# Strassen's seven products in the down-projection of a linear-attention and feed-forward layer, one Trainium2 core

## The chip, the core and the metric

The kernel runs on one core of a Trainium2 chip. Times are device microseconds (us) of one launch. The kernel before took 235.34 us (median of 3 runs, 234.85 to 235.41). The profile shows one further execution, whose instructions span 232.8 us. The 2.54 us between that span and the median lie around the instructions that the profile lists.

Five engines work side by side, each through its own queue in order: TensorE (PE, with its weight loads PEld), VectorE (DVE), ScalarE (ACT), GpSimd (POOL) and SyncE (SP), which here only issues DMAs.

## What is computed

The reference is one layer on 2048 tokens of width D = 640 in bf16: a pre-normed linear attention with 32 heads of 20, whose feature map is two softmaxes per head, and a pre-normed feed-forward block with F = 1728 hidden units.

```python
h = x + attention(layernorm(x), wqkv, w_phi, wo)
def _B_ref(x, w1, w2):
    h = jnp.einsum("bsd,df->bsf", x, w1)
    h = _silu(h)
    out = jnp.einsum("bsf,fd->bsd", h, w2)
    return out
h2 = h + _B_ref(_layernorm(h, axis=-1), B_w1, B_w2)
```

The change sits in the last product, silu(...) @ w2.

## The kernel before

The 2048 tokens are 16 tiles of 128. F is cut into 13 full chunks of 128 and a last one of 64. X stays in memory as 16 tiles of 128x640; the residuals are added into it.

**Order.** Nothing is scheduled while the program is built. Each piece of work is a named step (`add(name, emit)`, L212), and the list `ORDER` (L18 to L56) says in which order the steps are emitted (loop at L929). An engine gets its instructions in that order; between engines only data and buffers decide.

**Steps by name**, t being the tile. First half of the list: `K`, `V`, `kv` project keys and values and sum their products over all tiles. Then per tile: `Q` (L630, PE, 10 matmuls) projects queries, `qe` takes exponentials on ACT, `qs` sums them on DVE (L660), `qr` scales them on DVE (L690, from tile 6 on with a reciprocal L676 and ratio L682 before it), `qt` transposes by DMA (L702), `D` (L728) multiplies by the summed keys and values, `E` divides on DVE (two halves, L739), `ot` transposes by DMA, `G` (L764) is the output projection (two halves of 320 columns, 5 matmuls each), `ga` adds the residual on DVE (L772), `ls`, `lr`, `hn` are the layer norm: statistics on DVE (L430), the inverse root on POOL (L437, L443 and L446), the scaling on DVE (L448); `ht` transposes by DMA.

**Feed-forward.** The tiles are grouped in units: tiles 0 and 1, then 2 to 5, 6 to 9, 10 to 13, then 14 and 15 (L777). `u{a}.{f}` (L843) is an up-projection of the unit that starts at tile a: 5 matmuls of 512 columns for one hidden chunk of a unit of four tiles, or 10 of 256 for two chunks of a unit of two. `s` applies silu on ACT (L866) into the tile `shT`, hidden chunk by hidden chunk, tokens along the free axis. `u.L`, `s.L` and `lt` do the last 64 hidden units and transpose them. `d{t}{g}` (`ffn_down`, L884) is the down-projection of tile t for one half g of the 640 columns: 13 matmuls of 320 columns (L890) and one for the last 64 units (L893), accumulated in one bank. For tile 15 the second half is cut into 192 and 128 columns (`groups`, L807). `oa` (`ffn_out`, L895, L899) adds the bank and X on DVE into an output tile, of which there are two; `out` (L903) stores it.

**Banks.** From the step `halves` on (L706), the eight PSUM banks are handed out in a ring (`ps_half`, L121): a new use of a bank waits until the eighth use before it has been read.

**Memory.** The pool `late` (L837), which holds `shT` and the output tiles, takes the place of the pool `proj` (normalized rows, key, value and query weights) when the last exponentials `qe15` have been emitted. The key and value buffers EK and VP (L195, L197) lie in the pool `persist` and stay to the end.

Of the kernel before, what the change touches and what calls it, by code (L numbers as in the profile page):

```python
# [35 lines left out]
hn0 lr1 ot3 Q15 G20 hn1 ht1 qs6 G21 qe15 qs7 ht0 D5 G30 load8 pad1 ga20 qr6 ga21 ga30 G31 load11 E50 E51  # L36
D4 u0.12 E40 u0.4 u0.0 s0.0 s0.12 ga31 ls3 u0.6 E41 ot5 qs8 u0.L u0.2 ls2 qr7 s0.6 u0.8 qt6 lr2 s0.4 ot4
u0.10 D6 s0.L G50 s0.10 G40 lt0 qt7 lr3 s0.8 E60 G51 E61 s0.2 d10 ot6 ga40 hn2 ga50 ga51 ls5 hn3 lr5 G41
d00 D7 d01 ga41 ls4 G60 lr4 hn5 G61 E70 ht2 ht3 hn4 oa10 ht5 d11 qr8 oa00 ht4 ga61 u2.2 u2.0 ga60 qt8
E71 ot7 s2.0 oa01 qs9 u2.L qs13 s2.2 qr9 oa11 qs11 u2.6 D8 u2.10 E80 ls6 qt9 u2.7 u2.3 s2.L u2.11 s2.10  # L40
s2.6 qr13 E81 u2.9 s2.9 qr11 u2.5 qs12 s2.7 qs10 s2.3 u2.1 D9 G70 s2.5 E90 qr10 u2.12 s2.11 E91 ot8 G71
u2.4 lr6 ga71 ga70 qt11 out0 lt2 s2.1 qt10 u2.8 out1 hn6 s2.4 qr12 ls7 G80 s2.8 ga80 ot9 G81 D11 s2.12
E110 d30 ht6 qt13 E111 d20 D10 ga81 lr7 G90 E100 oa30 oa20 E101 ot10 G91 hn7 ga91 d31 ot11 ga90 ls8 qs15
lr8 d21 qt12 oa31 d50 G100 ls9 G101 hn8 out3 d40 d51 ht8 lr9 hn9 oa21 ga101 G110 out2 ga100 ga110 oa50
oa40 G111 qs14 d41 oa51 D12 ls10 ht7 E120 ht9 u6.1 u6.0 oa41 ga111 u6.12 u6.8 D13 s6.0 s6.1 qr14 s6.8
E121 s6.12 u6.11 ot12 u6.2 u6.3 qr15 lr10 s6.11 u6.L s6.2 E130 ls11 out4 E131 u6.9 qt15 s6.3 G120 ot13
s6.L u6.6 lt6 s6.6 lr11 u6.7 u6.10 hn10 u6.5 out5 s6.7 hn11 s6.9 u6.4 qt14 G121 ga120 ga121 s6.5 ht11
G130 D14 G131 E140 ga131 s6.10 s6.4 d60 ls12 oa60 d61 d70 ht10 lr12 E141 d91 ga130 ls13 oa61 hn12 oa70
D15 lr13 d90 ht12 ot14 d71 hn13 ht13 out6 G140 oa71 oa90 u10.L oa91 ga140 out9 E150 u10.0 u10.1 out7
E151 u10.6 G141 u10.9 s10.L s10.0 s10.6 u10.8 ga141 d80 u10.7 s10.1 u10.3 u10.11 ot15 s10.3 u10.5 u10.12  # L50
oa80 s10.9 s10.8 s10.11 u10.2 u10.4 ls14 s10.7 s10.5 u10.10 s10.12 s10.4 G150 G151 lt10 lr14 d81 s10.10
s10.2 d110 hn14 oa81 ht14 out8 d111 ga150 d120 ga151 ls15 d101 lr15 d100 hn15 oa100 oa110 ht15 oa101
d121 oa111 out10 oa120 out11 u14.L u14.4 u14.0 oa121 s14.0 s14.L u14.8 u14.6 s14.6 u14.2 d131 u14.12
# [6 lines left out]
def kernel(  # L60
# [151 lines left out]
    def add(name, emit):  # L212
        steps[name] = emit
# [680 lines left out]

    def ffn_out(t, g):  # L895
        if g == 0:
            outs[t] = pools["late"].tile([P, D], BF16, name="o_t", bufs=2)
        a, b = groups(t)[g]
        nc.vector.tensor_tensor(  # L899
            outs[t][:, a:b], ps_of.pop(("d", t, g))[:, 0 : b - a], X[:, t, a:b], op=ALU.add,  # L900
        )
# [24 lines left out]

    late = f"qe{T - 1}"
# [39 lines left out]
```

## Time and profile before

| what | value |
|---|---|
| median of 3 runs | 235.34 us |
| span of the profiled execution | 232.8 us |
| PE busy | 228.0 us, 1977 matmuls |
| DVE busy | 164.0 us, 340 instructions |
| ACT busy | 107.4 us, 241 instructions |
| POOL busy | 62.6 us, 99 instructions |
| down-projection matmuls of 320 columns (L890) | 403, 59.3 us |
| output additions of 320 columns (L899) | 31, 14.2 us |
| mean granted TensorE clock | 1.000 |

How to read it: each engine's share of the span is an average over stages. A matmul's own duration (299 ns for 320 columns) is longer than the distance to the next one, because matmuls are pipelined; what one costs in a row of them is the length of the row over its count. The chain that ended last leads back from the last instruction to whatever released each step. The windows show the busy time of each engine in a stretch of the span.

### The profile page before, as it was taken

Reading aid. Unit: us, or ns where it says so; the run is one execution under the profiler, and the core shown is the slowest. Engines: PE = TensorE matmul, PEld = TensorE weight load, DVE = VectorE, ACT = ScalarE, POOL = GpSimd, SP = SyncE. Lnnn points to the kernel's source line nnn. Section 1 sums busy time; section 2 is a strip of 40 time slices with the busy share of each in tenths; the row PEclk is TensorE's granted clock in tenths of the full one; section 3 lists DMA queues with packets and bytes.
Section 4 is the critical chain, followed back from the end, with each engine's and each line's share of the span. In section 5 each row is a group of like instructions: output and inputs, shape, how many; then the busy total and the mean of one; then the engine's idle time right before and its main releaser. Section 6 shows DMA issues by size and latency. Waiting matters only on the chain.

```text
span 232.8 us, 5040 instructions
## 1 busy us (share of the span) xinstructions
PE 228.0 (98%) x1977; PEld 160.5 (69%) x1984; DVE 164.0 (70%) x340; ACT 107.4 (46%) x241; POOL 62.6 (27%) x99
## 2 busy tenths in 40 slices
PE   7999999999999999999999999999999999999995
PEld 5777777777777778877545777655677455778874
DVE  4989999999999899998999794891472330404031
ACT  2899999998879884410344000064200235001400
POOL 7589896995001120211010111110020010100000
PEclk9999999999999999999999999999999999999999
DMA  6995379698836766696236956137213301011011
GB/s 169 336 291 103 87 119 217 217 145 188 220 115 114 159 116 136 124 121 146 56 66 154 120 114 158 30 80 172 55 28 85 99 0 28 31 28 56 8 56 56
DMA packets 67213, 26.79 MB, mean 115 GB/s; under 512 B 60151, under 2 KB 66167, under 8 KB 67063
## 3 DMA queue, kind: packets, MB, share of 16 engines
q1 hardware_dynamic: 66535, 26.47, 49.9%
q8 instruction: 15, 0.25, 0.5%
q10 hardware_dynamic: 656, 0.03, 0.2%
q14 instruction: 7, 0.06, 0.1%
HBM read 9.64 MB, written 2.62 MB: 53 GB/s over the span
## 4 chain that ended last, share of the span: by engine, by line
PE 95%; DMA 2%; SPq 1%; issue 1%; ACT 1%; DVE 0%
PE banks L890 24%; PE banks L850 24%; PE banks L498 18%; PE banks L536 9%; PE banks L767 9%; PE banks L589 2%; PE banks L734 2%; PE banks L893 2%; DMA Wk<-in_A_wqkv_dram 2%; PE banks L861 1%; PE banks L525 1%; PE banks L400 1%; ACT Wfk L325 1%; SPq L166 1%; PE banks L510 0%
## 5 line engine op out<-in xcount | busy, mean ns | idle before, releaser
L870 ACT ACTIVATE shT<-banks 128x512 bf16<-128x512 f32 (+1 forms) x53 | 28.5, 591 | 84.2 <-PE banks L850 84.2
L890 PE MATMUL banks<-w_sb,shT 128*128 128x320 bf16 (+2 forms) x429 | 61.3, 295 | 0.0
L850 PE MATMUL banks<-HnT,w_sb 128*128 128x512 bf16 (+1 forms) x318 | 58.4, 335 | 0.4
L890 PEld LDWEIGHTS <-shT 128*128 128x128 bf16 x429 | 41.1, 98 | 15.2
L850 PEld LDWEIGHTS <-w_sb 128*128 128x128 bf16 x325 | 31.2, 98 | 22.1
L899 DVE TENSOR_TENSOR o_t<-banks,X 128x320 bf16<-128x320 f32 (+2 forms) x33 | 14.9, 474 | 39.6 <-PE banks L893 26.7
L443 POOL TENSOR_SCALAR rs<-mv 128x1 f32<-128x1 f32 x21 | 5.8, 276 | 113.2 <-DVE mv L435 113.2
L498 PEld LDWEIGHTS <-XnT 128*128 128x128 bf16 x300 | 28.5, 98 | 10.3
L450 POOL TENSOR_SCALAR xn<-X,mv,rs 128x640 bf16<-128x640 bf16 x12 | 31.3, 2615 | 4.1 <-ACT rs L441 2.1
L434 DVE BATCH_NORM_STATS2 st<-X 128x6 f32<-128x320 bf16 x64 | 27.9, 477 | 4.3 <-DMA X<-in_A_x_dram 4.0
L767 PE MATMUL banks<-wo_sb,OT 128*128 128x320 bf16 x160 | 24.8, 299 | 0.0
L662 DVE TENSOR_REDUCE Sq<-EQ 128x66 f32<-128x1320 bf16 x16 | 23.9, 1512 | 0.0
L774 DVE TENSOR_TENSOR X<-banks,X 128x320 bf16<-128x320 f32 x32 | 14.7, 483 | 13.0 <-PE banks L767 12.9
L658 ACT ACTIVATE EQ<-banks 128x360 bf16<-128x360 f32 (+2 forms) x52 | 22.0, 514 | 3.2 <-PE banks L536 3.1
L557 DVE TENSOR_REDUCE Sk<-EK 128x64 f32<-128x1280 bf16 x16 | 23.3, 1468 | 0.2 <-ACT EK L553 0.2
L536 PE MATMUL banks<-Wfq,XnT 128*128 128x360 bf16 (+2 forms) x160 | 23.3, 299 | 0.0
L498 PE MATMUL banks<-Wv,XnT 128*128 128x320 bf16 x150 | 22.5, 299 | 0.0
L498 PE MATMUL banks<-Wfk,XnT 128*128 128x320 bf16 x150 | 22.5, 299 | 0.0
L553 ACT ACTIVATE EK<-banks 128x640 bf16<-128x640 f32 x32 | 20.5, 698 | 1.4 <-PE banks L498 1.2
L767 PEld LDWEIGHTS <-OT 128*128 128x128 bf16 x160 | 15.2, 98 | 6.5
L536 PEld LDWEIGHTS <-XnT 128*128 128x128 bf16 x160 | 15.2, 97 | 6.2
L747 DVE TENSOR_TENSOR O<-banks,Rd 128x360 bf16<-128x360 f32 (+1 forms) x32 | 15.7, 491 | 1.1
(76 smaller groups left out, 203.0 us busy)
## 6 DMA issues: line engine op xcount, KB each, us to landing
out_dram<-o_t SPq DMA_DIRECT2D x15, 160.0 KB, 2.0
w_sb<-in_B_w_dram SPq DMA_DIRECT2D x5, 432.0 KB, 4.8
w_sb<-in_B_w_dram SPq DMA_DIRECT2D x3, 480.0 KB, 4.1
X<-in_A_x_dram SPq DMA_DIRECT2D x1, 1280.0 KB, 8.4
Wk<-in_A_wqkv_dram SPq DMA_DIRECT2D x5, 160.0 KB, 3.8
Wv<-in_A_wqkv_dram SPq DMA_DIRECT2D x5, 160.0 KB, 4.9
wo_sb<-in_A_wo_dram SPq DMA_DIRECT2D x1, 800.0 KB, 6.5
X<-in_A_x_dram SPq DMA_DIRECT2D x1, 640.0 KB, 5.9
```

Of the source, the lines that this page charges most:

```text
L434: nc.vector.bn_stats(st[:, i, :], X[:, t, i * HD : (i + 1) * HD])
L450: eng.tensor_scalar(out=xn_[t][:], in0=X[:, t, :], scalar1=mv_.pop(t)[:, 0:1], scalar2=rs_.pop(t)[:], op0=ALU.subtract, op1=ALU.mult,)
L498: nc.tensor.matmul(ps[:, g, 0:HD], XnT[:, c, t * P : (t + 1) * P], W[:, c, g * HD : (g + 1) * HD], start=(c == 0), stop=(c == C - 1),)
L536: nc.tensor.matmul(ps[:, 0 : e - a], XnT[:, c, t * P : (t + 1) * P], Wfq[:, c, a:e], start=(c == 0), stop=(c == C - 1),)
L553: nc.scalar.activation(E5[:, :, :, b, :], p4, AF.Exp, scale=sign)
L557: nc.vector.tensor_reduce(sk[t][:], ek[t][:, 0 : H * HF].rearrange("p (q f) -> p q f", f=DH), axis=AX.X, op=ALU.add)
L658: nc.scalar.activation(features(t, a, b)[:, :, :, i], p4, AF.Exp, scale=sign)
L662: nc.vector.tensor_reduce(sq[t][:], EQ[0][:, t, :, 0:FCH].rearrange("p c (q f) -> p c q f", f=DH), axis=AX.X, op=ALU.add)
L767: nc.tensor.matmul(ps[:, 0:HD], ot[t][:, c, :], wo_sb[:, c, g * HD : (g + 1) * HD], start=(c == 0), stop=(c == C - 1),)
L850: nc.tensor.matmul(ps[:, at : at + n], w1_sb[:, c, fc * P : fc * P + P], HnT[u][:, c, 0:n], start=(c == 0), stop=(c == C - 1),)
L870: nc.scalar.activation(shT[u][:, f0 * n : f1 * n], ps_of.pop(("u", u, f0))[:, 0 : (f1 - f0) * n], AF.Silu)
L890: nc.tensor.matmul(ps[:, 0 : b - a], shT[u][:, at : at + P], w2_sb[:, fc, a:b], start=(fc == 0), stop=False,)
```

## The change

For tiles 2 to 15, taken in seven pairs, twelve of the thirteen full hidden chunks are multiplied by Strassen's scheme in Winograd's form. The two tiles are the two row blocks, chunks 0 to 5 and 6 to 11 the two inner blocks, columns 0 to 319 and 320 to 639 the two column blocks. Instead of eight block products (two tiles, two inner blocks, two column blocks) there are seven, `p1` to `p7`, of 6 matmuls each. The thirteenth chunk and the last 64 hidden units are multiplied as before (`rest`, at the end of p2, p3 and p4 and as `p8`). The seven products go into four banks, a to d, of which a takes p1, p6, p5 and a rest in turn and d takes p7 and p4; in between DVE reads the bank. Tiles 0 and 1 keep `d` and `oa`.

New work around the products:

- `T1` to `T4`, three steps each: sums of blocks of w2, once, on POOL, 128x640 each.
- `S1` to `S4` per pair: sums of blocks of `shT`, 128x768 each. S1 and S3 run on POOL, S2 and S4 on DVE; S2 needs S1, S4 needs S2. Each has one buffer.
- `r1`, `r2`, `r3`, `r7` per pair on DVE: bank plus X into an f32 tile of 128x320.
- `w11`, `w12`, `w21`, `w22` per pair on DVE: bank plus such a tile into the output tile.
- In the last pair p3 and w12 are cut at column 192 of the half; the stores of tile 14 come in three parts (columns 0 to 319, 320 to 511, 512 to 639), that of tile 15 in one.

There are four output tiles instead of two. VP and EK move into a pool that is closed together with `proj`. The list `ORDER` is rewritten from the step after `ga10` on; up to there it is the same.

```diff
-ga00 qe10 ga10 qt3 Q11 D3 qr4 qt5 ls0 G11 qe11 Q14 Q12 E30 Q13 lr0 ot2 qe14 ga11 qe12 qe13 ls1 qt4 E31
...
+ga00 qe10 ga10 qt3 Q11 D3 qr4 ot2 qt4 pad1 qt5 load11 ls0 G11 load8 qs7 qe11 Q14 qe14 lr0 Q12 G21 ga11
...
+lt0 lr5 hn2 ls4 hn5 ht2 E70 s0.8 ht5 ht3 u0.6 lr4 D8 E80 E71 T2.1 hn4 E81 s0.0 qs9 s0.6 d10 qr9 qs11
+T2.2 ht4 d11 d00 G60 oa10 G61 d01 u2.L T2.0 oa11 oa00 oa01 ot7 T3.0 s2.L qt9 ga61 u2.9 ga60 u2.0 u2.4
...
+qr13 ga111 qr12 S3.2 s2.11 p1.2 lr8 s2.10 qt13 p7.2 G110 r1.2 S1.2 S2.2 hn7 S3.4 r7.2 p6.2 out0 r2.2
+S4.2 p4.2 ht6 ga90 G100 ga91 w21.2 hn8 ls9 p5.2 qt12 G101 r3.2 p3.2 ga100 lr9 p8.2 ht8 ht7 S1.4 ga110
+hn9 p2.2 w22.2 D13 D12 ht9 ga101 w11.2 p2.4 E130 w12.2 ls10 p1.4 p7.4 u6.L r1.4 E131 S2.4 u6.2 S4.4 p6.4
...
+S4.10 lt14 r7.10 s14.10 p4.10 p5.10 S1.12 S3.12 r3.10 w21.10 p2.10 w11.10 p8.10 w22.10 s14.0 s14.8 p3.10
+S2.12 p1.12 s14.12 u14.6 r1.12 S4.12 s14.6 p7.12 out8 p6.12 p2.12 w12.10 S3.14 r7.12 r2.12 w11.12 p5.12
+r3.12 p4.12 p3.12 S1.14 S2.14 p1.14 p7.14 r1.14 p8.12 w21.12 out10 w22.12 p6.14 r7.14 r2.14 out11 p2.14
+w11.14 out140 p5.14 p4.14 S4.14 w12.12 p3.14x r3.14 p8.14 p3.14 out12 w21.14 w12.14x w22.14 w12.14 out13
+out142 out15 out141
...
+    keys = proj_ctx.enter_context(tc.tile_pool(name="keys", bufs=1, side="right"))
...
-    VP = [persist.tile([P, H, HV], BF16, name=f"VP{i}") for i in range(NV)]
-    EK = [persist.tile([P, FCH * (NCH - 1) + P], BF16, name=f"EK{i}") for i in range(NE)]
+    VP = [keys.tile([P, H, HV], BF16, name=f"VP{i}") for i in range(NV)]
+    EK = [keys.tile([P, FCH * (NCH - 1) + P], BF16, name=f"EK{i}") for i in range(NE)]
...
+    KS = (FC - 2) // 2
...
+    def weight_sum(k, c):
+        if k not in ws:
+            ws[k] = pools["late"].tile([P, KS, HD], BF16, name=f"T{k}")
+        (b11, b12), (b21, b22) = halves_of_w2()
+        x, y = {1: (b12, b11), 2: (b22, ws.get(1)), 3: (b22, b12), 4: (b21, ws.get(2))}[k]
+        part = slice(2 * c, 2 * c + 2)
+        nc.gpsimd.tensor_tensor(ws[k][:, part], x[:, part], y[:, part], op=ALU.subtract)
...
+    def token_sum(t, k):
+        S_[t, k] = pools["late"].tile([P, KS, P], BF16, name=f"S{k}", bufs=1)
+        a11, a12, a21, a22 = (block(t + i, j) for i in range(2) for j in range(2))
+        x, y, op = {
+            1: (a21, a22, ALU.add), 2: (S_.get((t, 1)), a11, ALU.subtract),
+            3: (a11, a21, ALU.subtract), 4: (a12, S_.get((t, 2)), ALU.subtract),
+        }[k]
+        eng = engines[on(f"S{k}.{t}", ("DVE", "POOL")[k % 2])]
+        eng.tensor_tensor(S_[t, k][:], x if k in (1, 3, 4) else x[:], y[:] if k == 4 else y, op=op)
+
+    FIRST = {1: "a", 2: "c", 3: "b", 7: "d"}
+    INTO = {1: "a", 2: "c", 3: "b", 4: "d", 5: "a", 6: "a", 7: "d"}
+    OTHER = {2: (0, 0), 3: (0, 1), 4: (1, 0)}
...
+    def product(t, k, lo=0, hi=HD):
+        bank = INTO[k] + "x" * (lo > 0)
+        if k in FIRST:
+            ps_of[bank, t] = ps_half()
+        ps = ps_of[bank, t]
+        (b11, b12), (b21, b22) = halves_of_w2()
+        left = {
+            1: lambda: block(t, 0), 2: lambda: block(t, 1), 3: lambda: S_[t, 4], 4: lambda: block(t + 1, 1),
+            5: lambda: S_[t, 1], 6: lambda: S_[t, 2], 7: lambda: S_[t, 3],
+        }[k]()
+        right = {1: b11, 2: b21, 3: b22, 4: ws.get(4), 5: ws.get(1), 6: ws.get(2), 7: ws.get(3)}[k]
+        for c in range(KS):
+            nc.tensor.matmul(
+                ps[:, lo:hi], left[:, c, :], right[:, c, lo:hi], start=(c == 0 and k in FIRST),
+                stop=(c == KS - 1 and k not in OTHER), skip_group_check=True,
+            )
+        if k in OTHER:
+            i, g = OTHER[k]
+            rest(ps, t + i, g, lo, hi)
+
+    def kept(t, name, bank, i, g):
+        r_[t, name] = pools["late"].tile([P, HD], F32, name=name, bufs=1)
+        nc.vector.tensor_tensor(
+            r_[t, name][:], ps_of[bank, t][:, 0:HD], X[:, t + i, g * HD : (g + 1) * HD], op=ALU.add
+        )
+
+    def added(t, name, bank, i, g, lo=0, hi=HD):
...
+        nc.vector.tensor_tensor(
+            outs[t + i][:, g * HD + lo : g * HD + hi], ps_of[bank, t][:, lo:hi], r_[t, name][:, lo:hi], op=ALU.add
+        )
```

More of the change, by code (lines that the diff above doesn't have):

```diff
@@ L39 @@
[L39 to L53, printed above, removed]
@@ L807, in groups @@
     def groups(t):
-        return ((0, 320), (320, 512), (512, 640)) if t == T - 1 else ((0, 320), (320, 640))
+        return ((0, 320), (320, 640))
     for t in range(T):
@@ L896, in ffn_out @@
         if g == 0:
-            outs[t] = pools["late"].tile([P, D], BF16, name="o_t", bufs=2)
+            outs[t] = pools["late"].tile([P, D], BF16, name="o_t", bufs=4)
         a, b = groups(t)[g]
@@ new lines, in kept @@
+    def kept(t, name, bank, i, g):
[4 more added lines that the diff above has]
+    def added(t, name, bank, i, g, lo=0, hi=HD):
+        if t + i not in outs:
+            outs[t + i] = pools["late"].tile([P, D], BF16, name="o_t", bufs=4)
+        nc.vector.tensor_tensor(
+            outs[t + i][:, g * HD + lo : g * HD + hi], ps_of[bank, t][:, lo:hi], r_[t, name][:, lo:hi], op=ALU.add
+        )
@@ new lines @@
+    PAIRS = range(2, T, 2)
+    for k in range(1, 5):
+        for c in range(KS // 2):
+            add(f"T{k}.{c}", lambda k=k, c=c: weight_sum(k, c))
+    for t in PAIRS:
+        for k in range(1, 5):
+            add(f"S{k}.{t}", lambda t=t, k=k: token_sum(t, k))
+        last = t == T - 2
+        cuts = ((0, 192), (192, HD)) if last else ((0, HD),)
+        for k in range(1, 8):
+            if k != 3:
+                add(f"p{k}.{t}", lambda t=t, k=k: product(t, k))
+        for j, (lo, hi) in enumerate(cuts):
+            add(f"p3.{t}" + "x" * j, lambda t=t, lo=lo, hi=hi: product(t, 3, lo, hi))
+            add(f"w12.{t}" + "x" * j, lambda t=t, lo=lo, hi=hi: added(t, "r3", "b" + "x" * (lo > 0), 0, 1, lo, hi))
+        add(f"p8.{t}", lambda t=t: rest(ps_of["a", t], t + 1, 1, 0, HD))
+        add(f"r1.{t}", lambda t=t: kept(t, "r1", "a", 0, 0))
+        add(f"r2.{t}", lambda t=t: kept(t, "r2", "a", 1, 0))
+        add(f"r3.{t}", lambda t=t: kept(t, "r3", "a", 0, 1))
+        add(f"r7.{t}", lambda t=t: kept(t, "r7", "d", 1, 1))
+        add(f"w11.{t}", lambda t=t: added(t, "r1", "c", 0, 0))
+        add(f"w21.{t}", lambda t=t: added(t, "r2", "d", 1, 0))
+        add(f"w22.{t}", lambda t=t: added(t, "r7", "a", 1, 1))
```

53 lines of the change are left out of this document (41 added, 12 removed).

## The prediction

> **What bounds the kernel now.** I read the page's engine shares and slices first, then the chain that ended last, then the windows by stage. The page:
>
> ```profile
> span 232.8 us, 5040 instructions
> PE 228.0 (98%) x1977; PEld 160.5 (69%) x1984; DVE 164.0 (70%) x340; ACT 107.4 (46%) x241; POOL 62.6 (27%) x99
> PEclk9999999999999999999999999999999999999999
> PE 95%; DMA 2%; SPq 1%; issue 1%; ACT 1%; DVE 0%
> ```
>
> TensorE holds 95% of the chain at full clock, so every matmul that goes is worth its own length, as long as no other engine holds TensorE up. The windows say who could (us, then busy PE, PEld, DVE, ACT, POOL, clock, DMA):
>
> ```profile
> 80.00:100.00 20.00, 20.00 (x204) 16.09 (x203) 18.58 (x44) 12.45 (x31) 3.69 (x9) 1.00 0.62 125
> 100.00:120.00 20.00, 19.89 (x156) 12.47 (x157) 18.70 (x45) 2.45 (x5) 2.53 (x6) 1.00 0.56 100
> 120.00:140.00 20.00, 19.95 (x158) 13.24 (x158) 18.14 (x43) 4.73 (x9) 1.56 (x4) 1.00 0.67 126
> 160.00:180.00 20.00, 20.00 (x169) 13.49 (x167) 8.18 (x22) 3.36 (x6) 1.74 (x4) 1.00 0.32 76
> ```
>
> From 80 to 140 us VectorE has only 1.3 to 1.9 us of room in 20; from 160 on it has more than half. A gain on TensorE is safe late and doubtful early.
>
> **What goes.** The chain in order of time (start, length, line, matmuls):
>
> ```profile
> 100.66 1.77 PE banks L890 x13
> 102.43 0.14 PE banks L893
> 113.38 1.08 PE banks L850 x5
> 98.28 0.33 PE banks L734 x11
> 98.62 2.04 PE banks L767 x15
> 78.28 2.73 PE banks L536 x20
> 230.13 0.29 DVE o_t L899
> ```
>
> A down-projection matmul costs 1.77 / 13 = 0.136 us. Per pair 4 x 12 of them become 7 x 6; the rest (chunk 13 and the last 64 units) stays 4 x 2. So 6 x 0.136 = 0.82 us goes per pair, and seven pairs save **5.72 us**. The cut of tile 15 goes and one of p3 comes; that is even. At the end the last addition has 192 columns in place of the 128 that took 0.29 us; by the 0.48 us that 320 columns take (below), 64 more cost 0.06. Both the stores behind it are small; the 160 KB store of tile 15 starts about half a microsecond earlier than the last one. The weight loads run beside the matmuls and fall with them.
>
> **What comes on VectorE.** Start-to-start times are what an engine in a full row pays (start, length, line, form):
>
> ```profile
> 114.56 0.48 DVE L899 TENSOR_TENSOR o_t<-banks,X 128x320 bf16<-128x320 f32 x1
> 114.96 1.52 DVE L662 TENSOR_REDUCE Sq<-EQ 128x66 f32<-128x1320 bf16 x1
> 116.39 0.26 DVE L746 RECIPROCAL Rd<-banks 128x18 f32<-128x18 f32 x1
> 117.14 0.88 DVE L434 BATCH_NORM_STATS2 st<-X 128x6 f32<-128x320 bf16 x2
> 118.18 0.31 DVE L676 RECIPROCAL Rq<-Sq 128x33 f32<-128x33 f32 x1
> 119.20 0.24 DVE L746 RECIPROCAL Rd<-banks 128x14 f32<-128x14 f32 x1
> 119.84 0.35 DVE L676 RECIPROCAL Rq<-Sq 128x33 f32<-128x33 f32 x1
> 100.43 0.44 DVE L450 TENSOR_SCALAR xn<-X,mv,rs 128x640 bf16<-128x640 bf16 x1
> 100.78 0.88 DVE L774 TENSOR_TENSOR X<-banks,X 128x320 bf16<-128x320 f32 x2
> 78.09 1.27 DVE L774 TENSOR_TENSOR X<-banks,X 128x320 bf16<-128x320 f32 x3
> ```
>
> So an addition out of a bank costs 0.40, `qs` 1.43, the halves of `E` 0.75 and 0.64, `ls` 1.04, `qr` about 1.04, `hn` 0.35. The eight `r` and `w` of a pair have the form of the addition, with an f32 tile on one side: 0.40 each. For S2 and S4 (128x768, two bf16 tiles) I have two rows of the same kind, and for S1, S3 and the T sums on GpSimd one from each side (mean ns):
>
> ```profile
> L693 DVE TENSOR_TENSOR EQ<-EQ,Rho 128x660 bf16<-128x660 bf16 x16 | 8.1, 505 | 0.3
> L570 DVE TENSOR_TENSOR EK<-EK,Rk 128x1280 bf16<-128x1280 bf16 x16 | 13.5, 860 | 0.0
> L369 POOL TENSOR_TENSOR phi_q<-WPQ,own_q 120x600 bf16<-120x600 bf16 x1 | 1.3, 1328 | 0.0
> L450 POOL TENSOR_SCALAR xn<-X,mv,rs 128x640 bf16<-128x640 bf16 x12 | 31.3, 2615 | 4.1 <-ACT rs L441 2.1 <-DVE mv L435 0.9 <-DVE xn L450 0.8
> ```
>
> S2 and S4: 505 + 108 x (355 / 620) = 0.57 us long, about 0.48 start to start. On GpSimd 1.33 / 600 gives 2.2 ns an element: T 1.42, S 1.70 us. At the rate of the other row (2.62 / 640 = 4.1 ns) T is 2.6 and S 3.1. I take the first, as it is the same operation with two tiles in; the second stays as the upper end.
>
> VectorE pays 8 x 0.40 + 2 x 0.48 = 4.2 us a pair for 1.6 before, 18 us more over the kernel. From tile 6 on that falls into room. For pairs 2 and 4 it falls into the full stretch.
>
> **Does VectorE keep up?** I add up both engines from `ga00`, up to which the lists agree, to `w11` of the first pair. VectorE: 23 `ga`, 4 `oa`, 4 `r`, 3 `w` at 0.40, 10 `ls`, 8 `qs`, 9 `E` pairs, 9 `qr` (one short), 10 `hn`, 2 S: 61.3 us. TensorE: 5 `Q` at 1.37, 11 `D`, 21 `G` at 0.68, 13 `u` at 1.08 with `u2.L` (0.6) and the unit of two (7.4), 4 `d` at 1.90, the pair (6.7): 61.2 us. In the list of before, VectorE's 60.2 us up to `ga110` stand beside 66.4 us of TensorE, with 11 `d` ahead of it: 6 us of room are now none. `ga00` starts at 78.09; `Q11`, the second half of the row at 78.28, at 79.65. So TensorE would stand at 140.9 and VectorE at 139.4 plus its idle time. Checked on the row at 109.58 below, the sums are short: 28.6 for 31.5 elapsed, of which the windows count some 29.3 busy, so 3%, or 1.8 us here. That leaves VectorE 0.3 us late with no idle time at all. If the idle time of before (1.4 in 20) all came back, it would be 4.3 more; but most of that was waiting on a TensorE that had other work. I take 1.0 us of stall for this, with 0 and 4.6 as ends.
>
> ```profile
> 109.58 0.23 DVE L746 RECIPROCAL Rd<-banks 128x14 f32<-128x14 f32 x1
> ```
>
> **The new waits.** p6 stands behind r1 and S2, and S2 behind S1 on GpSimd. Behind S2 in VectorE's queue stand `hn`, r7, r2 and the residuals of the next tiles, and behind p6 on TensorE p4 and `G`. Between p1's end and p6 of the first pair lie p7 and `G110`, 1.5 us; r1 and S2 fit (0.9) if S1 is there. In pair 12, S1 has one buffer and waits for p5 of pair 10; p7 of pair 12 waits for S3 behind it: 2 x 1.70 + 0.3 of handovers = 3.7, against 4.36 of TensorE work between (p2, p8, p3, p1, `u14.6`). In pair 14, S1 and S2 need 2.6 after p5 of pair 12, against 4.1. With S at 1.70 these cost nothing. The 28 other bank reads lie beside a product of at least 0.82 us. `out0` to `out3`, which move ahead of transposes on SP, wait for additions at least ten VectorE steps older (4 us at 0.40). VP and EK freed with the other buffers delay nothing: their last readers end at 67.0 us in the row below, over 20 us of TensorE work ahead of the pool that follows. Four output tiles take away waits of VectorE only.
>
> ```profile
> 65.67 1.35 PE banks L589 x44
> ```
>
> **GpSimd against VectorE.** Twelve T and four S run inside VectorE's full stretch. The trace shows the two engines holding each other up:
>
> ```profile
> 26.97 2.50 POOL L450 TENSOR_SCALAR xn<-X,mv,rs 128x640 bf16<-128x640 bf16 x1
> 27.39 1.13 DVE L570 TENSOR_TENSOR EK<-EK,Rk 128x1280 bf16<-128x1280 bf16 x1
> 77.04 0.49 DVE L693 TENSOR_TENSOR EQ<-EQ,Rho 128x660 bf16<-128x660 bf16 x1
> 77.11 0.60 POOL L682 TENSOR_TENSOR Rho<-Sq,Rq 128x66 bf16<-128x66 f32 x1 [1.53 <-ACT Rq L674]
> 20.48 0.82 DVE L570 TENSOR_TENSOR EK<-EK,Rk 128x1280 bf16<-128x1280 bf16 x1
> 18.53 2.52 POOL L450 TENSOR_SCALAR xn<-X,mv,rs 128x640 bf16<-128x640 bf16 x1
> ```
>
> VectorE's two-tile operation at 27.39, begun 0.42 us into a GpSimd operation, takes 1.13 in place of 0.82; the one at 20.48, begun 1.95 us into one, is not delayed. GpSimd's at 77.11 stands until VectorE's has all but ended. So GpSimd holds something for its first 0.7 us of 2.5. How long a sum of two tiles holds it, no row shows: between that quarter and the whole. Candidates for a clash in list order: `hn4` and `qr9` beside seven T in a row after `lr4` (half a T, 0.7; then 1.4, since ratio and scale each meet one), `qr13` beside S1, `qr12` beside S3 of the next pair, `hn9` beside S1 of pair 4 (half an S, 0.85, each): 4.65 us at whole length. I take half, **2.3 us**.
>
> [...]
>
> **Sum.** Against the profiled run: 232.8 - 5.72 + 0.06 + 1.0 + 2.3 = 230.4; with the 2.54 us around the span **233.0 us**, 1% faster.
>
> **The rivals.**
> (a) GpSimd's sums don't clash: VectorE's operations slip between them. 233.0 - 2.3 = 230.7. For it speaks the row at 20.48, against it the one at 27.39.
> (b) The sums hold for their whole length: 233.0 + 2.35 = 235.35, the gain given back to the early stretch. For it speaks the row at 77.11. [...]
> (c) Slower: GpSimd's sums run at the rate of its `xn`, S at 3.1. It decides from S = 2.0 on, where pair 12's 2 S + 0.3 passes 4.36. At 3.1 that joint costs 2.1, S2 of the first pair comes 2 x 1.4 = 2.8 later, and the clashes double to 4.6: 229.7 + 1.0 + 2.1 + 2.8 + 4.6 = 240.2, or 235.6 without clashes; middle 238. For it speaks that this is GpSimd's nearest row by size, against it that that one does two operations with per-row scalars.
>
> **How the numbers follow.** Forecast 0.36 (231.7 to 234.4), (a) 0.17, (b) 0.18, (c) 0.25, something else 0.04. The forecast's own range takes half and double of the clashes' half. Less than 0.3%, or 0.7 us, can't be told from no change. Faster by more: forecast, (a) and a little of (b), 0.56; within: most of (b), 0.14; slower: (c), the top of (b) and the rest, 0.30. The range reaches from (a) with no stall from the sums nearly to the top of (c): 230.0 to 239.0.
>
> **What would show it.** Right: 48 fewer matmuls and PE busy near 222; VectorE at 19 or more in 20 from 80 to 160 us; waits of TensorE on VectorE and GpSimd of about 3 us, nearly all between 105 and 150; VectorE's `qr`, `hn` or S lengthened where a GpSimd sum runs; S at 1.7. Wrong: S above 2.0 us, waits in the late pairs (p6 or p7 on GpSimd), a chain through GpSimd, or a granted clock below 1.000 after a stall.

## The result, and the profile after

The changed kernel takes **237.26 us** (median of 4 runs, 236.43 to 237.52), where the kernel before took 235.09 (4 runs, 234.58 to 235.41) on the same chip: ratio **1.0096, 95% interval 1.0071 to 1.0120**. It is 1% slower. The forecast of 233.0 said 1% faster; the time lies inside the range on record, but on the wrong side of no change, and above the 235.35 of rival (b). (The 2.54 us that the forecast adds around the span hold some difference between executions: where time and span are of the same execution, 1.7 to 2.2 us lie around it. That does not touch the forecast change.) Page of the kernel after: span, busy time by engine, granted clock, and the chain that ended last.

```profile
span 234.7 us, 5028 instructions
PE 223.4 (95%) x1927; PEld 156.0 (66%) x1936; DVE 192.9 (82%) x382; ACT 108.6 (46%) x241; POOL 102.1 (44%) x125
PEclk9999999999999999999999999999999999999999
PE 63%; DVE 25%; issue 5%; DMA 3%; ACT 1%; POOL 1%; DVEq 0%; ACTq 0%; SPq 0%
```

TensorE has less to do (the 1936 weight loads are 48 fewer, as the lists say), at full clock, and yet the span is 1.9 us longer. The chain has moved: a quarter of it now runs over VectorE. The windows of the kernel after, with the columns as before (busy PE, PEld, DVE, ACT, POOL, then clock, DMA share, GB/s):

```profile
80.00:100.00 20.00, 18.93 (x190) 14.67 (x188) 19.41 (x45) 10.99 (x28) 4.38 (x6) 1.00 0.94 149
100.00:120.00 20.00, 18.62 (x170) 12.81 (x169) 19.59 (x42) 3.83 (x8) 14.55 (x16) 1.00 0.58 96
120.00:140.00 20.00, 17.52 (x120) 10.13 (x121) 19.20 (x42) 5.78 (x10) 10.10 (x11) 1.00 0.51 104
140.00:160.00 20.00, 19.03 (x162) 13.04 (x162) 19.54 (x44) 2.15 (x4) 3.15 (x5) 1.00 0.39 82
160.00:180.00 20.00, 19.21 (x147) 11.40 (x146) 15.09 (x35) 5.89 (x12) 7.35 (x9) 1.00 0.53 101
```

VectorE stands above 19 in 20 from 80 to 160 us, and TensorE, which had at most 0.11 us of holes in each of the windows shown of before, now has 0.8 to 2.5 in each. What TensorE waited for (total, times, longest, us):

```profile
PE banks L974 <- DVE S L945: 2.4, 1, 2.4
PE banks L741 <- DVE X L781: 1.0, 1, 1.0
PE banks L741 <- DVE o_t L992: 0.9, 1, 0.9
...
PE banks L741 <- DMA EqT<-EQ: 0.8, 1, 0.8
PE banks L974 <- DVE r L985: 0.7, 1, 0.7
```

With 0.57 at 115.47, on the half down-projection's addition, these six waits come to 6.3 us. So the saving came and was spent. To see both, I measure every kernel from here on also by a **late stage**: from the start of the last common piece of the two orders (the row of twenty matmuls that holds Q11) to the end of the last matmul. The two rows that bound it, in the timeline of TensorE of the kernel after:

```profile
78.03 2.90 PE L543 MATMUL banks<-Wfq,XnT 128*128 128x360 bf16 x20
...
231.57 0.25 PE L958 MATMUL banks<-w_last,shT_l 128*128 128x192 bf16 x1
```

231.82 - 78.03 = 153.79 us. For the kernel before, whose rows are these,

```profile
78.12 2.90 PE L536 MATMUL banks<-Wfq,XnT 128*128 128x360 bf16 x20
...
229.87 0.22 PE L893 MATMUL banks<-w_last,shT_l 128*128 128x128 bf16 x1
```

it is 230.09 - 78.12 = 151.97. The difference of 1.82 is 5.72 saved, 6.3 waited, and 1.2 more, which fits what a stop costs beyond its hole. The hole begins where the last matmul ends, 299 ns after its start for 320 columns; in a row the next one would have started 136 ns after it. So each stop costs 0.16 us more than the list counts, 1.0 us for six. The same rest in kernels of the experiments below is 0.16 to 0.18 us a stop: 0.68 us for the four of e1, 1.10 for the six of e12, 0.49 for the three of e5 (but 0.34 for the only one of e2).

**Why TensorE waits** shows in VectorE's timeline. Ten of its instructions take two to five times their length:

```profile
86.60 1.19 DVE L457 TENSOR_SCALAR xn<-X,mv,rs 128x640 bf16<-128x640 bf16 x1
88.10 1.03 DVE L689 TENSOR_TENSOR Rho<-Sq,Rq 128x66 bf16<-128x66 f32 x1
...
107.67 1.56 DVE L457 TENSOR_SCALAR xn<-X,mv,rs 128x640 bf16<-128x640 bf16 x1
...
112.00 1.58 DVE L700 TENSOR_TENSOR EQ<-EQ,Rho 128x660 bf16<-128x660 bf16 x1
...
133.50 1.82 DVE L700 TENSOR_TENSOR EQ<-EQ,Rho 128x660 bf16<-128x660 bf16 x1
...
136.28 1.82 DVE L700 TENSOR_TENSOR EQ<-EQ,Rho 128x660 bf16<-128x660 bf16 x1
...
144.66 1.65 DVE L457 TENSOR_SCALAR xn<-X,mv,rs 128x640 bf16<-128x640 bf16 x1
...
170.58 1.75 DVE L457 TENSOR_SCALAR xn<-X,mv,rs 128x640 bf16<-128x640 bf16 x1 [0.71 <-POOL rs L453]
...
174.87 1.71 DVE L945 TENSOR_TENSOR S<-S,shT 128x768 bf16<-128x768 bf16 x1
...
216.66 1.75 DVE L945 TENSOR_TENSOR S<-S,shT 128x768 bf16<-128x768 bf16 x1
```

and GpSimd's timeline has a sum at each of these places (start, length, line, count):

```profile
86.21 2.83 POOL L928 TENSOR_TENSOR T<-w_sb 128x640 bf16<-128x640 bf16 x2
...
106.30 4.18 POOL L928 TENSOR_TENSOR T<-w_sb,T 128x640 bf16<-128x640 bf16 x3
...
111.80 4.38 POOL L928 TENSOR_TENSOR T<-w_sb,T 128x640 bf16<-128x640 bf16 x3
...
133.26 1.70 POOL L945 TENSOR_TENSOR S<-shT 128x768 bf16<-128x768 bf16 x1
...
136.06 1.68 POOL L945 TENSOR_TENSOR S<-shT 128x768 bf16<-128x768 bf16 x1 [1.10 <-PE banks L974]
...
144.50 1.63 POOL L945 TENSOR_TENSOR S<-shT 128x768 bf16<-128x768 bf16 x1
...
170.51 1.64 POOL L945 TENSOR_TENSOR S<-shT 128x768 bf16<-128x768 bf16 x1
172.93 3.23 POOL L945 TENSOR_TENSOR S<-shT 128x768 bf16<-128x768 bf16 x2 [0.79 <-ACT shT L877]
...
214.76 3.24 POOL L945 TENSOR_TENSOR S<-shT 128x768 bf16<-128x768 bf16 x2 [8.95 <-PE banks L974]
```

Read one pair: the sum at 133.26 ends at 134.96; VectorE's scaling begins at 133.50 and ends at 135.32, 0.36 us after the sum. All ten end soon after the sum that they met, and each form always as long after it: `hn` 0.18 to 0.19 us, a ratio 0.09, a scaling 0.36, S2 0.42. However long before that end they began (0.94 to 1.57 us), they were held until it. Against the usual lengths (0.44 for `hn`, 0.23 for a ratio, 0.50 for a scaling, 0.55 for S2) the ten lose 11.3 us together, 7.6 of it in the seven up to 145 us. (The expectations below count eight and 8.8 us, without the `hn` at 170.58 and the S2 at 216.66.) The longest hole of TensorE is their consequence: two scalings in a row meet S1 of the first pair and S3 of the second, S2 stands behind both in VectorE's queue, and p6 behind S2.

```profile
139.02 0.99 PE L974 MATMUL banks<-T,S 128*128 128x320 bf16 x6 [2.37 <-DVE S L945]
```

### The profile page after: what moved, and what is told of

The parts are those of the page before. It is cut to its first block, busy times and chain, and to the rows that moved or that the text cites. A ratio compares the mean times of both kernels' runs of the same rounds, so it can differ in the third digit from the quotient of the medians.

```text
span 234.7 us, 5028 instructions
## 1 busy us (share of the span) xinstructions
PE 223.4 (95%) x1927; PEld 156.0 (66%) x1936; DVE 192.9 (82%) x382; ACT 108.6 (46%) x241; POOL 102.1 (44%) x125
## 4 chain that ended last, share of the span: by engine, by line
PE 63%; DVE 25%; issue 5%; DMA 3%; ACT 1%; POOL 1%; DVEq 0%; ACTq 0%; SPq 0%
PE banks L505 17%; PE banks L857 15%; PE banks L974 14%; DVE Sq L669 6%; DVE X L781 3%; DVE O L754 3%; PE banks L897 3%; DVE st L441 3%; PE banks L774 3%; PE banks L543 2%; PE banks L596 2%; DMA EqT<-EQ 2%; DVE EQ L700 2%; DVE xn L457 2%; DVE Rd L753 2%
## 5 line engine op out<-in xcount | busy, mean ns | idle before, releaser
L857 PE MATMUL banks<-HnT,w_sb 128*128 128x512 bf16 (+1 forms) x316 | 59.7, 335 | 1.0 <-DVE o_t L906 0.6
L877 ACT ACTIVATE shT<-banks 128x512 bf16<-128x512 f32 (+1 forms) x53 | 29.6, 589 | 61.0 <-PE banks L857 59.0
L945 POOL TENSOR_TENSOR S<-shT 128x768 bf16<-128x768 bf16 x14 | 22.9, 1644 | 23.2 <-PE banks L974 16.5
L985 DVE TENSOR_TENSOR r<-banks,X 128x320 f32<-128x320 f32 x28 | 13.5, 484 | 16.2 <-PE banks L974 16.1
L774 PE MATMUL banks<-wo_sb,OT 128*128 128x320 bf16 x160 | 25.3, 299 | 0.1
L974 PEld LDWEIGHTS <-S 128*128 128x128 bf16 x174 | 16.6, 98 | 10.2 <-DVE S L945 3.4
L974 PE MATMUL banks<-T,S 128*128 128x320 bf16 x126 | 20.2, 299 | 3.1 <-DVE S L945 2.4
L992 DVE TENSOR_TENSOR o_t<-banks,r 128x320 bf16<-128x320 f32 (+2 forms) x29 | 13.4, 473 | 10.0 <-PE banks L958 9.4
```

The source lines that it names most:

```text
L774: nc.tensor.matmul(ps[:, 0:HD], ot[t][:, c, :], wo_sb[:, c, g * HD : (g + 1) * HD], start=(c == 0), stop=(c == C - 1),)
L857: nc.tensor.matmul(ps[:, at : at + n], w1_sb[:, c, fc * P : fc * P + P], HnT[u][:, c, 0:n], start=(c == 0), stop=(c == C - 1),)
L877: nc.scalar.activation(shT[u][:, f0 * n : f1 * n], ps_of.pop(("u", u, f0))[:, 0 : (f1 - f0) * n], AF.Silu)
L945: eng.tensor_tensor(S_[t, k][:], x if k in (1, 3, 4) else x[:], y[:] if k == 4 else y, op=op)
L974: nc.tensor.matmul(ps[:, lo:hi], left[:, c, :], right[:, c, lo:hi], start=(c == 0 and k in FIRST), stop=(c == KS - 1 and k not in OTHER), ...
```

## The experiments

The theory after seeing this (A): the sums on GpSimd hold VectorE's two-tile operations and `hn` for their whole length, and in VectorE's full stretch each such loss comes back as a wait of TensorE. Rival (B): the new order and VectorE's additional additions are too much by themselves, and the clashes only show where time would be lost anyway. All ratios are to the kernel before on the same chip.

**1. Leave sums out.** In e1 the products read plain blocks of `w2` for T; in e2 and e13 they read plain blocks of the hidden values for S, in e2 plain blocks for T as well. These kernels leave out work that the layer needs; matmuls, additions and order stay.

```diff
...
-        nc.gpsimd.tensor_tensor(ws[k][:, part], x[:, part], y[:, part], op=ALU.subtract)
+        ws[k] = {1: b12, 2: b22, 3: b22, 4: b21}[k]                                # e1, e2
...
-        eng.tensor_tensor(S_[t, k][:], x if k in (1, 3, 4) else x[:], y[:] if k == 4 else y, op=op)
+        S_[t, k] = {1: block(t + 1, 0), 2: block(t, 0), 3: block(t, 0), 4: block(t, 1)}[k]   # e2, e13
```

e1, no weight sums. 

> The weight sums T are left out: the products read plain blocks of w2 in their place; all else is the changed kernel. Theory A (a sum of two tiles on GpSimd holds an access to memory that VectorE's two-tile operations and its hn need, for the whole 1.4 or 1.64 us): the four VectorE operations that ran beside a T (hn1 1.19, the ratio of tile 6 1.03, hn4 1.56, the scaling of tile 9 1.58 us) go back to 0.44, 0.23, 0.44, 0.50; TensorE's gaps at 88 to 92 and at 114 us (1.1 and 0.6) go and the one at 136 to 140 (2.4) shrinks by about 1: 234.6 us, between 233.8 and 235.6. Theory B (VectorE is simply too full with its own additions and sums; GpSimd only happens to run then): no T was on VectorE, so 237 us, within 0.5.

e2, no sums at all. 

> All sums T and S are left out: the products read plain blocks of w2 and of silu's output; r and w stay. A: no VectorE operation is lengthened; TensorE keeps only the 0.75 us gap at 103 us (a transposition by DMA that landed late): 231.3 us, between 230.5 and 232.3. B: of VectorE's 4.2 us per pair only 1.0 goes, 2 us in its full stretch, so at most 2 us better: 235 to 236.5.

e13, weight sums only. 

> The token sums S left out (products 3, 5, 6 and 7 read plain blocks of the hidden values), the weight sums T kept on GpSimd. With all sums left out the kernel took 231.1, with S alone 233.9, with both 237.3. If the two kinds of sums cost independently, T alone costs 3.4: 234.5 (233.9 to 235.2), with the same four operations lengthened up to 113 us and a late transposition of tile 8 at 103. If VectorE catches up with the delay of T when no S follow, less: 232.0 to 233.8. If GpSimd's sums each cost their own length in VectorE's row whatever stands behind, 236 or more.

| kernel | T | S | median us | ratio (95%) | late stage us |
|---|---|---|---|---|---|
| after | yes | yes | 237.26 | 1.0096 (1.0071 to 1.0120) | 153.79 |
| e1 | no | yes | 233.87 | 0.9958 (0.9942 to 0.9974) | 151.01 |
| e13 | yes | no | 233.16 | 0.9903 (0.9878 to 0.9928) | 150.90 |
| e2 | no | no | 231.14 | 0.9839 (0.9820 to 0.9858) | 147.46 |

Without its sums the change is worth 1.6%: B's 235 to 236.5 for e2 falls, and so does its 237 for e1. As e2 has the new order and VectorE's additions, these two together cost less than the products save. No instruction of VectorE is lengthened there, and TensorE waits once by over 0.3 us in the late stage, for a DMA transposition of an attention output at 91.5 us (0.87 us). 151.97 - 147.46 = 4.51 gained, with 0.87 of this wait 5.4: the saving of 5.72 is there within 0.3. In e1 the four operations up to 113 us have their usual lengths and six beside the token sums are long (1.94, 1.59, 1.67, 1.75, 1.70 and 1.75 us). In e13 it is the other way round, and TensorE waits five times up to 119 us, 3.8 us in all, then no more; its time is in the range given for a VectorE that catches up. Whether the two costs add up is not settled: by the stage they do nearly (3.44 and 3.55 alone, 6.33 together), by the ratios T costs 0.64%, S 1.19% and both 2.57%, so that the delay of T would partly be caught up where no S follow. The stage is of one execution, and e13's profiled one (233.66) is among its slower.

**2. The token sums on VectorE.** e3 puts S1 and S3 there too; e12 does so with the weight sums left out as in e1; e8 puts all sums there.

```diff
-        eng = engines[on(f"S{k}.{t}", ("DVE", "POOL")[k % 2])]
+        eng = engines[on(f"S{k}.{t}", "DVE")]                                      # e3, e8, e12
...
-        nc.gpsimd.tensor_tensor(ws[k][:, part], x[:, part], y[:, part], op=ALU.subtract)
+        nc.vector.tensor_tensor(ws[k][:, part], x[:, part], y[:, part], op=ALU.subtract)   # e8
```

e3. 

> S1 and S3 run on VectorE instead of GpSimd; the result is the same. VectorE gets 0.48 us more per sum, 1.9 us in its full stretch. A: the four clashes with S go (scaling of tiles 13 and 12, 1.82 each for 0.50; hn9 1.65 for 0.44; S2 of the pair at tile 6 1.75 for 0.55: 5.0 us), so VectorE is 3 us earlier at 147 us, and TensorE's gaps at 136 to 140, 146 and 176 us shrink from 3.9 us to about 1: 234.5 us, between 233.6 and 235.6. B: VectorE is fuller, 238 to 239.5 us.

e12. 

> The weight sums T left out (products read plain blocks of w2), and S1 and S3 on VectorE with S2 and S4. With T left out and the S as they are the kernel took 233.9, with all sums left out 231.1: the token sums cost 2.7 us. If that is the clashes of GpSimd's S with VectorE, moving them to VectorE leaves 4 S of 0.55 us in the full stretch and a chain S1, S2 without a clash: 232.2 (231.6 to 232.9), no lengthened operation. If it is the work and its order itself (S in front of p6 and p7), nothing is won: 233.5 to 234.3. If a load of VectorE weighs more than its length, above 234.3.

e8. 

> The changed kernel with all T and S on VectorE, none on GpSimd. No clash is left, but VectorE gets 12 x 0.41 + 4 x 0.48 = 6.8 us more in its full stretch, for 8.8 us of lengthening that goes. A: about 2 us less lateness, 235.5 us, between 234.3 and 237. B (VectorE's own load is the cause): worse than the changed kernel by 4 us or more, 241.

e12 came out as the clashes have it: 232.80, ratio 0.9901 (0.9871 to 0.9932), stage 149.82. It does more work on VectorE than e1 and is 0.6% faster. No operation is lengthened, its S stand at the length of any two-tile operation (VectorE's timeline),

```profile
132.83 0.55 DVE L941 TENSOR_TENSOR S<-shT 128x768 bf16<-128x768 bf16 x1
```

and p6 waits 0.41 us for S2, where it waited 1.79 in e1. e3 was a miss: 236.20, ratio 1.0056 (1.0035 to 1.0077), stage 153.40. The six clashes of S are gone and p6's wait falls from 2.37 to 0.42, but the four clashes of T stand as before, and a wait of 1.18 us at 118.97 for the transposition of a scaled query tile has come. e13, which has T and no S, shows it too:

```profile
119.23 0.51 PE L741 MATMUL banks<-KVB,EqT 128*128 128x63 bf16 x11 [1.40 <-DMA EqT<-EQ]
```

I read this as a VectorE that T has put behind and that has nothing left with which to carry two more S; no run takes the two apart. e8 was just above its range: 237.29, ratio 1.0123 (1.0094 to 1.0151). It has no clash at all, but VectorE carries T itself, and p6 waits again, 2.1 us. Of its four executions, the two of 237.76 and 238.19 have a mean granted clock of 0.993, the two of 236.26 and 236.82 one of 1.000; these two stand 0.6 to 0.9% above the median of before, e3 0.6%. So in VectorE's full stretch the T cost about as much by their own length as by their clashes. B's 241 falls here as well, but its idea holds this far: what counts in this stretch is VectorE's time, whether a sum runs on it or holds it up.

**3. What of a GpSimd instruction holds VectorE?** e4 replaces each T by a constant write of 1536 elements, which takes nearly as long (1.38 to 1.44 us in the rows below, a T 1.38 to 1.46 in the kernel after) and reads nothing (the weight sums then hold a constant).

```diff
...
-        nc.gpsimd.tensor_tensor(ws[k][:, part], x[:, part], y[:, part], op=ALU.subtract)
+        at = (0, 384, 0)[c]
+        nc.gpsimd.memset(ws[k][:].rearrange("p c e -> p (c e)")[:, at : at + 1536], 0.5)
```

> The weight sums are left out: at each of their places GpSimd writes a constant into 1536 elements of the T tile, about 1.4 us each, and reads nothing. A in its narrow form (what is held is reading): two-tile operations of VectorE (ratio of tile 6, scaling of tile 9) are at 0.23 and 0.50; time near that without T, 234.6 us, between 233.8 and 235.8. A in its wide form (any GpSimd access holds it): as the changed kernel, 237 us within 0.5. B: 237 us.

It took 235.40, ratio 1.0019 (0.9999 to 1.0040), stage 152.99: in the range of the narrow form, the wide one falls. GpSimd's timeline, then VectorE's:

```profile
87.33 2.87 POOL L926 MEMSET T<- 128x1536 bf16 x2
...
101.21 1.38 POOL L926 MEMSET T<- 128x1536 bf16 x1
...
106.57 8.38 POOL L926 MEMSET T<- 128x1536 bf16 x6
```

```profile
87.73 1.15 DVE L457 TENSOR_SCALAR xn<-X,mv,rs 128x640 bf16<-128x640 bf16 x1
...
89.19 0.23 DVE L689 TENSOR_TENSOR Rho<-Sq,Rq 128x66 bf16<-128x66 f32 x1
...
107.96 1.61 DVE L457 TENSOR_SCALAR xn<-X,mv,rs 128x640 bf16<-128x640 bf16 x1
...
112.07 0.23 DVE L689 TENSOR_TENSOR Rho<-Sq,Rq 128x66 bf16<-128x66 f32 x1
112.33 0.50 DVE L700 TENSOR_TENSOR EQ<-EQ,Rho 128x660 bf16<-128x660 bf16 x1
```

The ratios and the scaling, which take two tiles in, run at their usual length (0.23 and 0.50 us) in the middle of a write; `hn`, one bf16 tile in and one out, takes 1.15 and 1.61 us for 0.44. Counted by the mean length of a write in its row (1.44 and 1.40 us), it ends 0.1 and 0.2 us after the write, beside a sum 0.18 to 0.19. The kernel before has such a case already, the second of two `hn` in a row beside the one constant write in its late stage (VectorE, then GpSimd); it ends 0.18 us after the write:

```profile
84.62 0.69 DVE L450 TENSOR_SCALAR xn<-X,mv,rs 128x640 bf16<-128x640 bf16 x1
```

```profile
84.51 0.62 POOL L237 MEMSET w_last<- 64x640 bf16 x1
```

So what is held differs by form in these rows: a two-tile operation only beside a GpSimd instruction that reads (the scaling took 0.50 us beside a write, 1.58 beside a sum), `hn` beside either (1.61 us beside a write, 1.56 beside a sum). Why the two forms differ, no row shows.

**4. The sums without the change.** e5 is the kernel before, with its own down-projection and its own order, and with the twelve T and four of the S issued on GpSimd at places like those of the changed order and used by nobody (the key and value buffers go to the pool that is freed early, for room).

```diff
+    for k in range(1, 5):
+        for c in range(KS // 2):
+            add(f"T{k}.{c}", lambda k=k, c=c: weight_sum(k, c))
+    for t in (2, 4):
+        for k in (1, 3):
+            add(f"S{k}.{t}", lambda t=t, k=k: token_sum(t, k))
```

> The kernel before, with its own down-projection, and beside it on GpSimd the twelve T sums and four S sums of tiles 2 to 5 at about the places of the changed kernel; nobody reads them (VP and EK in the freed pool make room). A (a GpSimd sum holds VectorE's two-tile operations and hn for its length): some of VectorE's scalings, ratios and hn take 1.0 to 1.8 us, in all 3 to 6 us more; before has about 5 us of room in that stretch, so the time goes up by 0.3 to 2.5 us: 236.3. B: nothing depends on the sums, VectorE's instructions keep their lengths, 234.9 within 0.4.

236.54, ratio 1.0091 (1.0058 to 1.0125), stage 154.09, which is 2.1 over before. Nobody waits for these sums, so what they cost comes by lengthened instructions of VectorE or by an `rs` that stands behind them in GpSimd's queue (0.75 us, in the second row below). Seven VectorE instructions are lengthened, by 5.8 us in all, for instance

```profile
109.22 1.59 DVE L695 TENSOR_TENSOR EQ<-EQ,Rho 128x660 bf16<-128x660 bf16 x1
...
144.34 1.75 DVE L452 TENSOR_SCALAR xn<-X,mv,rs 128x640 bf16<-128x640 bf16 x1 [0.75 <-POOL rs L448]
```

**5. The new order alone.** e11 has the changed order with plain half down-projections in place of the products, and no sums.

```diff
-    PAIRS = range(2, T, 2)
-    for k in range(1, 5):
+    PAIRS = range(T, T, 2)
+    for k in ():
...
-            if t < 2:
+            if t < T:
```

(with `p`, `r`, `w`, S and T taken out of the order and `d` and `oa` put in their places)

> The new list without Strassen: all tiles with d and oa (the halves where the list had the products, the additions where it had r and w), no T, no S, four output tiles. TensorE has the 48 matmuls again. A (the loss comes from the clashes, the list costs only late transpositions early): before plus 0.5 to 1.5 us, 235.8. If the list is itself the cause of the loss (7.6 us of it in the changed kernel): 238 or more.

239.21, ratio 1.0187 (1.0162 to 1.0213): far off what was expected. By the expectation it speaks for the list as the cause; but half down-projections of 1.9 us stand where products of 0.82 stood, so it is not the same order in time, and e2, which has the list with its products, is 1.6% faster than before. For the change it decides nothing. It does show the wait at 90 us for a transposition of an attention output, which e2 has too and the kernel before not:

```profile
90.44 1.53 PE L768 MATMUL banks<-wo_sb,OT 128*128 128x320 bf16 x10 [1.05 <-DMA OT<-O]
```

So 0.7 (e12) to 1.05 us can be lost here by the order, without any sum. In the changed kernel TensorE's wait at 90 us, 1.0 us long, is put down to a residual on VectorE instead.

**6. Strassen's products where VectorE has room.** Four kernels keep plain half down-projections for the early tiles, put all S on VectorE, and issue T late: e6 takes pairs 8 to 14 in the changed order, e7 pairs 6 to 14, e9 and e14 pairs 8 to 14 in the order of before up to E141, with T behind the statistics of tiles 9, 10, 11 and 13. In e9 two banks are taken again before their sums are read, so it does not compute the layer; e14 is the same with p1, p2, r1, w11, a half down-projection and an addition moved, so that each bank is kept. (All four are edits of the changed kernel.)

```diff
-    PAIRS = range(2, T, 2)
+    PAIRS = range(8, T, 2)                                        # range(6, T, 2) in e7
...
-            if t < 2:
+            if t < 8:                                             # t < 6 in e7
```

e6. 

> The seven products only for tiles 8 to 15 (four pairs), tiles 2 to 7 with d and oa as before at the places of the products; T on GpSimd after the layer norm statistics of tiles 11 and 13; S1 to S4 on VectorE. Four pairs save 3.3 us. A: no GpSimd sum runs before about 155 us, VectorE has room after, so nothing is given back there; left are the gaps by late transpositions (about 0.8): 232.4 us, between 231.5 and 233.4. If the list itself costs something else than these clashes, it is still there: 234 or more.

e7. 

> As the kernel with four pairs, but five pairs, tiles 6 to 15, and T begun after the statistics of tile 10, so that some T run while VectorE still has little room. A: 4.1 us saved, 0.8 lost to late transpositions and 0 to 1 to clashes of T with the scalings of tiles 14 and 15: 232.0 us, between 231.0 and 233.2. If the list costs something else: 234 or more.

e9. 

> Four pairs, tiles 8 to 15, as in the earlier kernel of that kind, but with the list of the kernel before up to the division of tile 14 (E141), T on GpSimd after the statistics of tiles 9, 10, 11 and 13, S on VectorE. A: 3.3 us saved; the list of before has no gap at 88 to 92 us (1.0 with the new list); the T clash with hn and scalings of tiles 10 to 15 where VectorE has 5 us of room or more: 232.4 us, between 231.5 and 233.5, some 0.8 better than with the new list. If the new list's early part cost nothing: 233.4, as that kernel.

e14. 

> The order of before up to the end of the ratios of tile 14, then Strassen's products for the four pairs of tiles 8 to 15, all token sums on VectorE, the weight sums on GpSimd behind the statistics of tiles 9, 10, 11 and 13: e9 with p1, p2 and r1 of the first pair moved behind S2 and the seventh half down-projection ahead of E151, so that no bank is taken again before its sum is read. Four pairs save 4 x 0.82 = 3.3 us; the clashes of the weight sums fall where VectorE has 1 to 8 us of room in 20. If only the place of the sums made the change slow, 232.4 (231.5 to 233.5), without an idle stretch of TensorE ahead of 140. If VectorE's work of the pairs costs the kernel wherever it stands, 235 or more.

| kernel | median us | ratio (95%) | late stage us |
|---|---|---|---|
| e6 | 233.47 | 0.9951 (0.9929 to 0.9972) | 150.84 |
| e7 | 240.48 | 1.0240 (1.0212 to 1.0267) | 157.98 |
| e9 | 233.21 | 0.9939 (0.9919 to 0.9960) | 150.26 |
| e14 | 233.71 | 0.9961 (0.9937 to 0.9985) | 150.73 |

e6 and e14 beat both kernels, by 0.4 to 0.5% against before and by 1.3 to 1.4% against after (the quotients of the ratios). The 235 or more of e14's rival falls. The order of before, which has no wait at 90 us, brought nothing that can be told from noise: e9 and e14 stand 0.1% to either side of e6. The clashes have not gone, they stand where VectorE has room (17.0 and 13.5 us busy in e14's windows from 140 and 160, for 19.5 and 15.1 after). Seven instructions of e14's VectorE are lengthened beside sums, by 6.0 us in all, for instance

```profile
173.78 1.51 DVE L455 TENSOR_SCALAR xn<-X,mv,rs 128x640 bf16<-128x640 bf16 x1
176.59 1.72 DVE L943 TENSOR_TENSOR S<-shT 128x768 bf16<-128x768 bf16 x1
```

and TensorE waits 0.84 us for the transposition of a late `hn`. e6 and e14 came 0.1 and 0.2 us above their ranges: of 4 x 0.82 = 3.28 saved, e14 has 1.24 left in the stage; three waits take 1.54 (0.84, 0.43 for an `r`, 0.26 for an `E`), and the last 0.5 fits three stops at 0.17. e7 was a plain miss. Its T stand on GpSimd ahead of the `rs` of tile 13, `hn` waits for that in VectorE's queue, and S2 and p6 behind `hn`:

```profile
170.91 1.50 DVE L455 TENSOR_SCALAR xn<-X,mv,rs 128x640 bf16<-128x640 bf16 x1 [3.46 <-POOL rs L451]
```

A wait of TensorE of 4.7 us on S follows, and with it a loss of clock. First the row of p6, then the window of 176 to 178 us, columns as before (the clock is the third number from the end):

```profile
174.13 1.78 PE L972 MATMUL banks<-T,S 128*128 128x320 bf16 x6 [4.70 <-DVE S L943]
```

```profile
176.00:178.00 2.00, 2.00 (x9) 1.19 (x8) 1.97 (x6) 0.00 (x0) 0.00 (x0) 0.50 0.42 113
```

The granted clock is 0.50 from 174 to 179 us, and six matmuls take 1.78 us for 0.98, so about 3 us go on top of the wait. The waits of 2.37 us after and of 2.1 in e8's profile have a clock of 1.00 behind them. GpSimd's small share of busy time (29.9 us from 78 us to the end) hides the cause of the wait: `rs` is short (0.22 and 0.57 us in the kernel after), but VectorE's queue waits 3.46 us for it.

## Why the prediction was wrong, point by point

- **42 matmuls x 0.136 = 5.72 saved: right.** e2 has 5.4 of it, with its one wait added back.
- **The end, + 0.06: right.** VectorE's last addition takes 0.36 us for the 0.29 of before.
- **VectorE too full by 1.0: right in size.** With all S on VectorE and no sum on GpSimd (e12), TensorE waits 1.3 us up to 140. Half of that is not the missing room at 135 to 140 that the working had in mind but a transposition at 90 (0.68), which the moved order brings; so the size came out partly by luck.
- **T and S by the two-tile row of GpSimd (1.42 and 1.70): right,** 1.40 and 1.64 measured. With that rival (c), whose price hung on S above 2.0, fell. So the time that (c) gave was near the measured one for a reason that did not happen. (The 0.3 of handovers there was the author's estimate; after, S1 of the last pair begins 0.08 us after the matmul that it waited for, and the first p6 0.06 us after its S2.)
- **The new waits cost nothing with S at 1.70: too low.** Even without clashes e12 waits 0.41 us at the first p6 and 1.4 for four reads of banks by `r` and `w` (0.20, 0.44, 0.32, 0.43), three of them after 170 us; no term had these. With clashes p6 waits 2.37, because S2 stands in VectorE's queue behind two scalings that are each held up.
- **"I take half, 2.3 us": this is the step that failed.** It failed twice over. The hold was taken between a quarter and the whole of a GpSimd sum, from a row of a *one-tile* operation with scalars; sums of two tiles held until their end in each of the ten cases. And the list of clashes, five places with 4.65 us at whole length (measured there: 6.0), missed five more: `hn1` and the ratio of tile 6 beside T at 86 us, `hn13` at 171, S2 of pair 6 at 175 and S2 of pair 12 at 217. Measured: 11.3 us of lengthening, and by after against e12 (which has the same products and S, without a sum on GpSimd) 1.95% or 4.6 us of time, by after against e2 6.0. With 4.6 in place of 2.3 the sum on record gives 235.3.
- **The other 2 us are not in the clashes.** Without its clash term the sum on record is 4.66 us faster than before; e12, which has no clash, is 0.99%, 2.3 us, faster. Its stage shows where that went: 2.47 us of waits and some 1.1 us for six stops, 3.6 in all, where the sum had 1.0. (e12 also carries S1 and S3 on VectorE, which the changed kernel does not, so not all of this need be in the changed kernel.)
- **Rival (b) had the hold right:** it lasted to the end of the sum in all ten cases. Its chance was 0.18, and its price of 4.65 was that of an incomplete list. The row at 77.11 of before spoke for it; the rows at 20.48 and 27.39, from which the forecast took a shorter hold, were of another form of instruction, a GpSimd operation with one tile in.
- **"What would show it":** the matmuls, VectorE at 19 in 20, S at 1.64 and the clock came as written. The waits came from 89 to 177 us and to 6.3 us, not 3 us between 105 and 150.

## What to carry to other kernels

Before work is put on GpSimd beside a full VectorE, list every two-tile operation and every bf16 `tensor_scalar` of VectorE that can fall into a GpSimd instruction with two tiles in (here a scaling took 1.82 us for 0.50, an `hn` 1.75 for 0.44, an S2 1.75 for 0.55), over the whole stretch in which both can stand, and charge each with all that is left of what it meets, and what is queued behind it too. A term whose two ends decide the sign of the forecast is not to be settled by the middle: take the rows of the same form (two tiles against two tiles), and let the rest go. Where an engine has no room, the same work can be worth doing later: Strassen's products pay here for the last four pairs (0.4 to 0.5%), and in none of the three placings of the sums that were tried for all seven (0.6 to 1.2% slower).

## What the runs showed of the hardware

- What VectorE was held by beside GpSimd differed by form: a VectorE operation of two tiles took 0.50 us beside a GpSimd instruction that only writes and 1.58 beside one that reads two tiles; `hn` took 1.15 and 1.61 beside writing ones, for 0.44 alone. In the ten cases of the kernel after, what was held ended 0.09 to 0.42 us after the sum, alike for one form.
- A stop of TensorE cost 0.16 to 0.21 us beyond its hole (six stops and 1.2 us after, three and 0.49 in e5), in e2 0.34. After one of 4.7 us (e7) the granted clock was 0.50 for some 5 us; after those of 2.37 and 2.1 us it stayed 1.00.
- The additions with one input in a bank were not lengthened anywhere, though GpSimd had sums in the same stretch: the 28 of L985 took 435 to 493 ns, the 32 residuals of L781 436 to 492, while the 16 scalings of L700 went from 492 to 1819. An addition of L985 at 173.82 (0.49 us) and one of L781 at 180.94 (0.48) lay wholly inside sums, which ran from 172.93 to 176.16 and from 180.58 to 182.22. The groups of VectorE in the kernel after, by form (shortest, median, longest ns, first and last start):

```profile
L985 DVE TENSOR_TENSOR r<-banks,X x28: 435/491/493, 138.0 to 230.0; 128x320 f32<-128x320 f32 x28
L700 DVE TENSOR_TENSOR EQ<-EQ,Rho x16: 492/502/1819, 54.6 to 162.8; 128x660 bf16<-128x660 bf16 x16
```

This view shows at once that a form met a clash: its longest is over three times its median. How many there were, only the timeline to its end shows.
